# Seven block products for four of the twelve hidden tiles in a gated-attention and mixer kernel

## The chip, the cores and the metric

One NeuronCore of a Trainium2 chip runs the whole kernel. The metric is the device time of one execution in microseconds; the kernel before takes 1113.02 us, the median of three runs.

## The reference, cut to what matters

For each of 8 batches of 3008 rows and 256 channels, an attention without softmax gates u, and the result x goes through a mixer over rows (tokens) and then over channels:

```python
scores = (1 / S) * z @ z.T                   # 3008 x 3008, d_qk = 64
x      = u * (relu(scores) ** 2 @ v)         # 3008 x 256
h      = relu(x.T @ w_tok1) @ w_tok2         # tokens: 3008 -> 256 -> 3008
u2     = x + h.T
out    = u2 + relu(u2 @ w_ch1) @ w_ch2       # channels: 256 -> 1536 -> 256
```

The change is in the last line: in `u2 @ w_ch1` (the first channel product), and in how the sums for the second one are made. Operands are bf16, sums f32.

## The kernel before, in words

**Tiles.** A batch's 3008 rows are cut into 6 blocks q of 512 (the last has 448). Channels stand on the partitions as two tiles of 128 (DT = 2), the 1536 hidden channels as 12 tiles of 128 (CHT = 12). The first channel product of one block is `ch1` (line 1149): for c2 = 0 to 5 it computes two of the 12 hidden tiles, r = 0 and 1, each as two matmuls of 128 x 128 weights by 512 columns into one bank (line 1162), four matmuls a piece; six pieces a block. ScalarE evacuates the two banks in one ReLU of 1024 columns into `h2pre` (line 1201).

**The second channel product** (`product`, line 1272) already is a two-by-two block scheme with seven products in place of eight. It splits the 12 hidden tiles in halves r, the rows of a block in halves m and the 256 outputs in halves h. VectorE makes four sums of quarters of `h2pre` for each third d of the hidden tiles (`make_sums`, line 1227, operations at 1241, 1246, 1250, 1253) into `hsum`; four sums of the weights lie in `w_mix_sb` (`mix_weights`, line 974). The seven products, k = 1 to 7, are 12 matmuls of 128 columns each (line 1298) into the banks xb and zb; between them VectorE collects partial results into `ro` (`collect`, line 1309, operation at 1334). A product that goes on adding in the same bank (6 after 1, 3 after 5, 7 after 6, 4 after 7) waits for the collection of the one before it. After the seventh collection the block is stored with one DMA from SP's queue (line 1339). The token product (`tok1`, line 1008) is such a scheme too, with sums from `x_sums` (line 908).

**Banks.** PSUM is used as four pairs of banks. A piece takes a free pair (`take_slot`); the pair comes back when the operation that evacuates it is done. During a block's products xb and zb hold two of the four pairs, the pieces of `ch1` share the rest.

**What sets the order.** The program is written out by a planner in the kernel's own code. `push` (line 364) queues an operation of ScalarE, VectorE or SP with a time at which it is ready, a duration and a priority; `run_engines` gives out the earliest. TensorE's work is in pieces, in lists that are taken from the front (`next_piece`, line 1525). The planner only fixes the order of each engine's instructions; on the chip each engine runs its own list in order and waits on semaphores.

In the mixer, the pieces of a block q stand in this order (line 1510): the second product's pieces k = 1 to 7, and where a 0 stands a `ch1` piece of the next block, c2 = 0 to 4; the sixth, c2 = 5, comes just before the next block's turn:

```python
(0, 0, 1, 2, 0, 6, 5, 0, 7, 3, 0, 4)
```

Blocks 0 to 2 of a batch run in one stretch after its token product, with the `ch1` pieces of blocks 1 to 3 in between; blocks 3 to 5 follow one batch later. Attention (scores at line 465, products with v at line 692) runs in between.

Of the kernel before, what the change touches and what calls it, by code (L numbers as in the profile page):

```python
# [57 lines left out]
def kernel(  # L58
# [29 lines left out]
    sb = ctx.enter_context(tc.tile_pool(name="sb", bufs=2))  # L88
    psum = ctx.enter_context(tc.tile_pool(name="psum", bufs=2, space=bass.MemoryType.PSUM))
# [7 lines left out]
    mark = consts.tile([P, 32], F32)  # L97
# [4 lines left out]
    w_mix_sb = consts.tile([P, 4, CHT // 2, P], BF16)  # L102
    w_sum_sb = consts.tile([P, 3, KT // 2, P], BF16)
    ident = consts.tile([P, P], BF16)

    zs = consts.tile([P, KT + 2, d_qk], BF16)
# [74 lines left out]
    def turn_on_pe(zr, zp):  # L181

        for t in range(GK):
            nc.tensor.matmul(  # L184
                zp[:, t, :], zr[:, t].rearrange("p h d -> p (h d)"), ident[:],
                start=(t == 0), stop=True, skip_group_check=True)
# [15 lines left out]
    def fill(n, bank):  # L202

        for _ in range(n):
            nc.tensor.matmul(
                bank, zero[:, :P], zero[:], start=True, stop=True, skip_group_check=True)
# [672 lines left out]
    def turn_x(b, q, t):  # L879
# [10 lines left out]
        push("dve", t + slack, 0.21, 0.36, lambda t: x_sums(b, q, t), first=-1,  # L890
# [17 lines left out]
    def x_sums(b, q, t):  # L908


        if q % 2 == 0:
            d_pairs[b, q] = new_pair(xd_home(b, q), [3, QW // P // 2, P], "d_pair")
# [4 lines left out]
        steps = [(d[:, 1], high[:, 1], low[:, 1]), (low[:, 1], low[:, 1], low[:, 0]),  # L917
                 (d[:, 0], high[:, 1], low[:, 1]), (d[:, 2], high[:, 0], d[:, 0])]
# [55 lines left out]
    def mix_weights(t):  # L974
# [5 lines left out]
        for c in range(2):  # L980
# [3 lines left out]
                (to[:, 0], low[:, :, 1, :], low[:, :, 0, :]),  # L984
                (to[:, 2], high[:, :, 1, :], low[:, :, 1, :]),
                (to[:, 1], high[:, :, 1, :], to[:, 0]),
                (to[:, 3], high[:, :, 0, :], to[:, 1])]

        def step(t):
            nc.vector.tensor_sub(*steps.pop(0))  # L990
# [5 lines left out]

    BORROW = 3
    VERY_LAST = (B - 1, NQ - 1, CHT // 2 - 1)
    ORDER_LAST = ((1, 2, 6, 5, 7, 0, 3, 4), (1, 2, 6, 5, 0, 7, 3, 0, 4))

    def add_mixer(b):
# [6 lines left out]
        def tok1(q, end):  # L1008
# [10 lines left out]
            for i in range(n):  # L1019
# [4 lines left out]
                    ((1, 1), w[:, j, 0, 1, :], xp[:, 1, i, 0, :]),  # L1024
                    ((0, 2), w_sum_sb[:, 1, j, :], d[:, 0, i, :]),
                    ((1, 2), w_sum_sb[:, 0, j, :], d[:, 1, i, :]),
                    ((0, 3), w_sum_sb[:, 2, j, :], xp[:, 1, i, 1, :]),
                    ((1, 0), w[:, j, 1, 1, :], d[:, 2, i, :]),
# [8 lines left out]
            if q == NQ - 1:  # L1037
                home = "fl" if b else "h2"

                def collect_a(t):  # L1040
# [20 lines left out]
                    def one_high(t):  # L1061
                        nc.vector.tensor_add(f[:, 1, :], a_ps[:, 0, 3, :], f[:, 4, :])
                        st["a"] = sb.tile([P, 2, D], BF16, tag="a", name="a_sb", bufs=1)
# [12 lines left out]
                    def relu_a(m, t):  # L1076
# [7 lines left out]
                        if len(made) == 2:  # L1084
                            recent[0] = to[:, :1]
                            if b:
                                release("fl", [1], max(made))
                            else:
                                live["h2"] -= 1

# [8 lines left out]
        def tok2(q, end):  # L1099
# [9 lines left out]
            def add(t):  # L1109
# [13 lines left out]
                u_done[q].t = t  # L1123
                st["turned", q] = push("sp", t, 1.25, 5.5, lambda t: turn_u2(q, t), first=1,
                                       room=lambda: has_room(("us",)) and (
                                           q <= HALF or goal[0] > (b, 1 + HALF)))
            ring.append((push("dve", end + 0.21, 1.12, 1.25, add, first=2), slot))

# [20 lines left out]
        def ch1(q, c2, borrowed, end):  # L1149
# [64 lines left out]
            if c2 == CHT // 2 - 1:  # L1214
                release("xT", xT_uses[q])

# [4 lines left out]
        def tiles_of(q, d, r, m):  # L1221

            n = pairs_of(q)
            return st["h2", q, d].rearrange("p (j r) w -> p j r w", r=2)[
                :, :, r, :2 * n * P].rearrange("p j (i m s) -> p j i m s", m=2, s=P)[:, :, :, m, :]

        def make_sums(q, d, t):
# [6 lines left out]
            def kind(k):  # L1234
                return sums["s"][:, k, :, :n, :]

            def add1(t):
                home, n_home = take_home(q)
                sums["s"] = sb.tile([P, 4, 2, 2, P], BF16, tag=home, name="hsum", bufs=n_home)
                st["sum", q, d] = sums["s"]  # L1240
                nc.vector.tensor_add(kind(0), tiles_of(q, d, 0, 1), tiles_of(q, d, 1, 1))  # L1241
                push("dve", t - 0.05, busy, busy + 0.15, add3, done=s_done[q, d, 2])
# [679 lines left out]
```

## Time and profile before

| | |
|---|---|
| runs, us | 1117.03, 1112.36, 1113.02; median 1113.02 |
| span of the profiled execution | 1110.5 us (the page gives no other time of this execution) |
| instructions | 27244 |
| busy share: TensorE, VectorE, ScalarE, GpSimd | 100%, 70%, 60%, 15% |
| evacuations at line 1201 | 287, mean 1008 ns |
| stores at line 1339, from SP | 47, median 338 ns of issue |

How to read it: PE is TensorE, DVE VectorE, ACT ScalarE, POOL GpSimd, SP the engine that issues most DMAs; PEld is TensorE's weight load, SPq and ACTq are the queues of SP and ScalarE, where a DMA's issue is listed that the busy times leave out. A row of a group has line, engine, operation, output and inputs, shapes, count, then busy time and mean ns, then the idle time ahead of them and what ended it. A row of the timeline has start, length (both us), engine, line and operation; consecutive ones are merged, with their count. A row of the waits has who waited for whom, total us, times, longest. A matmul's listed duration includes its passage through the array; the next one is issued earlier.

### The profile page before, as it was taken

Reading aid. Unit: us, or ns where it says so; the run is one execution under the profiler, and the core shown is the slowest. Engines: PE = TensorE matmul, PEld = TensorE weight load, DVE = VectorE, ACT = ScalarE, POOL = GpSimd, SP = SyncE. Lnnn points to the kernel's source line nnn. Section 1 sums busy time; section 2 is a strip of 40 time slices with the busy share of each in tenths; the row PEclk is TensorE's granted clock in tenths of the full one; section 3 lists DMA queues with packets and bytes.
Section 4 is the critical chain, followed back from the end, with each engine's and each line's share of the span. In section 5 each row is a group of like instructions: output and inputs, shape, how many; then the busy total and the mean of one; then the engine's idle time right before and its main releaser. Section 6 shows DMA issues by size and latency. Waiting matters only on the chain.

```text
span 1110.5 us, 27244 instructions
## 1 busy us (share of the span) xinstructions
PE 1105.7 (100%) x11073; PEld 683.8 (62%) x11073; DVE 782.5 (70%) x1888; ACT 669.4 (60%) x843; POOL 164.3 (15%) x382
## 2 busy tenths in 40 slices
PE   9999999999999999999999999999999999999998
PEld 3444575766557665576556865557655676556676
DVE  6889865975758857588566885578756777556775
ACT  7999555645854567545665456653666536743454
POOL 5320110221003110032100311003210120000100
PEclk9999999999999999999999999999999999999999
DMA  9999947796977969779697797967979678693222
GB/s 177 155 194 164 192 98 143 141 174 134 191 133 141 180 148 174 133 147 203 135 183 119 131 214 139 172 123 152 202 154 170 111 148 182 127 164 93 67 58 96
DMA packets 465725, 165.54 MB, mean 149 GB/s; under 512 B 433024, under 2 KB 448960, under 8 KB 465600
## 3 DMA queue, kind: packets, MB, share of 16 engines
q1 hardware_dynamic: 436208, 131.11, 58.6%
q0 software_dynamic: 28880, 32.32, 21.2%
q8 instruction: 86, 1.41, 0.5%
q10 hardware_dynamic: 512, 0.38, 0.1%
q14 instruction: 39, 0.32, 0.1%
HBM read 65.40 MB, written 24.64 MB: 81 GB/s over the span
## 4 chain that ended last, share of the span: by engine, by line
PE 99%; DMA 1%; issue 0%; POOL 0%; DVE 0%; POOLq 0%
PE acc L692 42%; PE hp L1162 22%; PE xb L1298 11%; PE zb L1298 8%; PE sc L465 6%; PE h_ps L1105 4%; PE a_ps L1031 3%; PE op L1398 2%; PE first_acc L609 1%; DMA v_sb<-in_v_dram 1%; PE zp L184 0%; PE up L1700 0%; DVE res L1433 0%; POOL ident masks.py:199 0%; POOL ident masks.py:197 0%
## 5 line engine op out<-in xcount | busy, mean ns | idle before, releaser
L1201 ACT ACTIVATE h2pre<-hp 128x1024 bf16<-128x1024 f32 (+1 forms) x287 | 278.5, 1008 | 204.0 <-PE hp L1162 171.5
L692 PEld LDWEIGHTS <-v_sb 64*128 64x128 bf16 x4418 | 246.3, 94 | 210.9
L692 PE MATMUL acc<-at,v_sb 64*128 64x512 bf16 (+1 forms) x2738 | 340.9, 375 | 0.0
L503 ACT ACTIVATE at<-sc 128x1024 bf16<-128x1024 f32 (+1 forms) x290 | 286.6, 1027 | 62.5 <-PE sc L465 54.8
L1162 PE MATMUL hp<-xT,w_ch_sb 128*128 128x512 bf16 (+1 forms) x1152 | 274.7, 375 | 0.0
L511 DVE TENSOR_TENSOR at<-at 128x1024 bf16<-128x1024 bf16 (+1 forms) x290 | 198.2, 687 | 103.8 <-ACT at L503 99.9
L692 PE MATMUL acc<-fl,v_sb 64*128 64x512 bf16 (+1 forms) x1680 | 192.5, 367 | 0.0
L1162 PEld LDWEIGHTS <-w_ch_sb 128*128 128x128 bf16 x1152 | 105.6, 98 | 98.1 <-issue 3.0
L1298 PEld LDWEIGHTS <-hsum 128*128 128x128 bf16 x2088 | 124.4, 98 | 18.2 <-issue 0.3
L465 PE MATMUL sc<-zT 64*128 64x512 bf16 (+1 forms) x732 | 131.8, 359 | 0.2 <-ACT zT L1750 0.2
L1298 PEld LDWEIGHTS <-h2pre 128*128 128x128 bf16 x1566 | 95.5, 98 | 20.1
L820 ACT COPY cp<-acc 128x512 f32<-128x512 f32 (+1 forms) x94 | 54.9, 584 | 77.8 <-PE acc L692 66.8
L826 DVE TENSOR_TENSOR cp<-acc,cp 128x512 f32<-128x512 f32 (+1 forms) x94 | 63.5, 676 | 50.7 <-ACT cp L820 50.1
L1241 DVE TENSOR_TENSOR hsum<-h2pre 128x512 bf16<-128x512 bf16 (+1 forms) x141 | 56.1, 402 | 40.7 <-ACT h2pre L1201 39.4
L491 ACT ACTIVATE at<-sc 128x512 bf16<-128x512 f32 (+3 forms) x152 | 56.2, 447 | 41.5 <-PE sc L465 41.0
L1298 PE MATMUL xb<-w_mix_sb,hsum 128*128 128x128 bf16 x1044 | 73.7, 219 | 0.0
L1334 DVE TENSOR_TENSOR ro<-xb,u_sb 128x256 f32<-128x256 f32 (+1 forms) x141 | 56.5, 401 | 22.5 <-PE xb L1298 20.5
L542 DVE TENSOR_TENSOR at<-at 128x512 bf16<-128x512 bf16 (+3 forms) x152 | 41.5, 321 | 38.2 <-ACT at L491 38.2
L465 PEld LDWEIGHTS <-zT 64*128 64x128 bf16 x732 | 42.8, 94 | 41.2 <-issue 3.6
L124 POOL CAST mark<-at 128x1 f32<-128x1 bf16 x24 | 8.2, 342 | 372.5 <-DVE at L511 372.5
L846 DVE TENSOR_TENSOR xT<-cp,uT 128x512 bf16<-128x512 f32 (+1 forms) x94 | 62.5, 665 | 0.9
L1253 DVE TENSOR_TENSOR hsum<-h2pre,hsum 128x512 bf16<-128x512 bf16 (+1 forms) x141 | 56.6, 401 | 2.3
(89 smaller groups left out, 968.4 us busy)
## 6 DMA issues: line engine op xcount, KB each, us to landing
out_dram<-ro SPq DMA_DIRECT2D x40, 512.0 KB, 3.0
v_sb<-in_v_dram POOLq DMA_DIRECT2D x40, 256.0 KB, 4.6
ur<-in_u_dram POOLq DMA_DIRECT2D x40, 256.0 KB, 4.9
w_tok_sb<-in_moe_w_tok_dram POOLq DMA_DIRECT2D x10, 256.0 KB, 10.7
zs<-in_z_dram POOLq DMA_DIRECT2D x35, 64.0 KB, 3.8
at<-at SPq DMA_TRANSPOSE x114, 2.4
out_dram<-ro SPq DMA_DIRECT2D x7, 256.0 KB, 3.5
fl<-at SPq DMA_TRANSPOSE x105, 4.7
```

What stands on the lines that cost most here:

```text
L465: nc.tensor.matmul(sc[:, r, c0:c1], zT[h, k:k + P], zT[h, m + c0:m + c1], start=True, stop=True)
L491: nc.scalar.activation(a3[:, i, c0:c1], sc[:, r, c0:c1], ACT.Relu, scale=inv_S)
L503: nc.scalar.activation(view, sv, ACT.Relu, scale=inv_S)
L511: nc.vector.tensor_mul(view, view, view)
L692: nc.tensor.matmul(o, vs[blk.b, g][rows, i, dh * P:(dh + 1) * P], rhs, start=(dh, h) not in blk.begun, stop=stop, skip_group_check=True)
L826: nc.vector.tensor_add(cp[:, :W], acc[:, 0, :W], cp[:, :W])
L846: nc.vector.tensor_mul(xT[:, dh, :full * P].rearrange("p (t s) -> p t s", s=P), acc[:, :full * P].rearrange("p (t s) -> p t s", s=P), uT[: ...
L1162: nc.tensor.matmul(hps[r % len(hps)][:, r, :W], w_ch1_sb[:, dc, cc * P:(cc + 1) * P], xT[:, dc, :W], start=(dc == 0), stop=(dc == DT - 1))
L1201: nc.scalar.activation(h2[:, :, :W], hp[:, :, :W], ACT.Relu)
L1253: nc.vector.tensor_sub(kind(3), tiles_of(q, d, 1, 0), kind(1))
L1298: nc.tensor.matmul(to[:, i * P:(i + 1) * P], lhs, weights[:, c2, :], start=(first_use and c2 == 0 and i == 0), stop=(c2 == CHT // 2 - 1), ...
L1334: nc.vector.tensor_add(res(m, h), source, us(m, h) if opening else res(m, h))
```

## The change

For the batches b > 0 and the blocks q = 1, 2, 3, the first four of the 12 hidden tiles (d = 0, the pieces c2 = 0 and 1) are computed by seven block products. The block's 512 columns are halved (m, 256 each), the two channel tiles k are the inner dimension's halves, and the four hidden tiles are halved to r = 0, 1 with two tiles j each. Each of the seven products is two matmuls of 256 columns. They are given in four stages a, b, c, d, all in one pair of banks, one bank for each r (both column halves m of a product's j lie side by side in its bank):

- a: a plain product into bank 0, a mixed one into bank 1. ScalarE then copies bank 1 to a tile `s5` (`keep`) and copies bank 0 over bank 1 (`fork`).
- b: one more product into each bank. ScalarE evacuates bank 1 with a ReLU (`relu_first`) and forks again.
- c: one more into each bank. VectorE adds `s5` to both banks, with a clamp at 0, into half of `h2pre`, one operation of 1024 columns (`add_two`, the custom operation TENSOR_ADD_SAT).
- d: a last product into bank 1, evacuated by ScalarE with a ReLU (`relu_last`).

A stage waits for the work named behind the stage before it. The four mixed blocks of activations are made by VectorE in three operations per block (`token_quarters`: one of 512 columns, two of 256) into a tile `t_sums`, the mixed weights once in four operations (`hidden_weights`). The order of pieces of a block ahead of a grouped one becomes `GROUPED`; the three 0s are c2 = 2, 3, 4.

The forms of the sums change everywhere: `make_sums` makes three operations (one twice as wide) in place of four, and `x_sums` three in place of four; the signs of the weight sums and the places of the products 3, 4, 6, 7 change with them. The stores of the blocks are issued by ScalarE (`nc.scalar.dma_start`), put in its list when the planner has the last collection done. Memory: the mixed weights share one tile with the z rows, the identity shares one with the zeros, the ReLU of the token product lies in the tile of its sums, which is released after the last token piece instead of before the first.

```diff
+    HID, MIX = 8 * P, 4 * (CHT // 2) * P
+    shared_sb = consts.tile([P, HID + KT * d_qk + MIX], BF16)
+    w_hid_sb = shared_sb[:, :HID].rearrange("p (k j c) -> p k j c", k=4, c=P)
+    w_mix_sb = shared_sb[:, HID + KT * d_qk:].rearrange("p (k c d) -> p k c d", k=4, d=P)
+    zs = shared_sb[:, HID - d_qk:HID + (KT + 1) * d_qk].rearrange("p (t d) -> p t d", d=d_qk)
...
-        steps = [(d[:, 1], high[:, 1], low[:, 1]), (low[:, 1], low[:, 1], low[:, 0]),
-                 (d[:, 0], high[:, 1], low[:, 1]), (d[:, 2], high[:, 0], d[:, 0])]
+        steps = [(d[:, 0:2], v[:, 1].rearrange("p j r d -> p r j d"), low),
+                 (d[:, 2], high[:, 1], d[:, 0]), (d[:, 3], high[:, 0], d[:, 2])]
...
+    def hidden_weights(t):
+        w1 = w_ch1_sb[:, :, :4 * P].rearrange("p k (j r c) -> p r k j c", r=2, c=P)
+        to = w_hid_sb
+        steps = [
+            (nc.vector.tensor_add, to[:, 0], w1[:, 1, 0], w1[:, 1, 1]),
+            (nc.vector.tensor_sub, to[:, 1], to[:, 0], w1[:, 0, 0]),
+            (nc.vector.tensor_sub, to[:, 2], w1[:, 0, 0], w1[:, 1, 0]),
+            (nc.vector.tensor_sub, to[:, 3], w1[:, 0, 1], to[:, 1])]
...
+    GROUPED = ("a", 0, 1, 2, "b", 6, 5, 0, "c", 7, 3, 0, 4, "d")
...
+        def grouped(q, d=0):
+            return b > 0 and 0 < q <= HALF and d == 0
...
+        def token_quarters(q):
+            xT = xTs[b, q]
+            quarter = xT.rearrange("p k (m n) -> p k m n", m=2)
...
+                nc.vector.tensor_sub(tile_["T"][:, 0:2], quarter[:, :, 1], quarter[:, 0])
...
+                nc.vector.tensor_sub(T[:, 2], quarter[:, 1, 1], T[:, 0])
...
+                nc.vector.tensor_sub(T[:, 3], quarter[:, 1, 0], T[:, 2])
...
+        def grouped_ch1(q, d, stage, end):
...
+            products = [
+                [(0, w1[:, 0, 0], x[:, 0, 0], True), (1, w_hid_sb[:, 0], T[:, 0], True)],
+                [(1, w1[:, 0, 1], x[:, 1, 0], False), (0, w_hid_sb[:, 1], T[:, 2], False)],
+                [(0, w_hid_sb[:, 3], x[:, 1, 1], False), (1, w_hid_sb[:, 2], T[:, 1], False)],
+                [(1, w1[:, 1, 1], T[:, 3], False)]][stage]
+            for r, lhs, rhs, begins in products:
+                for j in range(2):
+                    nc.tensor.matmul(
+                        ps[:, r, j * 2 * P:(j + 1) * 2 * P], lhs[:, j, :], rhs,
+                        start=begins and j == 0, stop=True, skip_group_check=True)
...
+            def fork(t):
+                nc.scalar.copy(half(1), half(0))
+            def keep(t):
+                nc.scalar.copy(s5, half(1))
+                push("act", t - 0.16, 0.62, 0.78, fork, first=2, done=g_done[q, d, 0])
+            def relu_first(t):
+                nc.scalar.activation(h[:, 0, 0], half(1), ACT.Relu)
+                push("act", t - 0.16, 0.62, 0.78, fork, first=2, done=g_done[q, d, 1])
+            def relu_last(t):
+                nc.scalar.activation(h[:, 1, 0], half(1), ACT.Relu)
...
+            def add_two(t):
+                nc.vector._custom_dve(
+                    TENSOR_ADD_SAT, out=h[:, :, 1, :], in0=ps,
+                    in1=s5.unsqueeze(1).to_broadcast([P, 2, QW]), s0=3.0e38, s1=0.0)
+                make_sums(q, d, t, last=h2_done[q, 2 * d])
...
-                nc.vector.tensor_add(kind(0), tiles_of(q, d, 0, 1), tiles_of(q, d, 1, 1))
+                nc.vector.tensor_sub(sums["s"][:, 0:2, :, :n * P], h[:, :, 1], h[:, 0])
...
-                    nc.sync.dma_start(
-                        out=rows_of(out[b], q)[:, :2 * n, :], in_=st["res", q][:, :2 * n, :])
-                    free["sp"] = max(free["sp"], t) + 0.4
-                    release(home_of(q), [1], t + 4.0)
+                    push("act", t, 0.1, 0.1, store, first=1)
                     release("us", us_uses[q])
+
+            def store(t):
+                nc.scalar.dma_start(
+                    out=rows_of(out[b], q)[:, :2 * n, :], in_=st["res", q][:, :2 * n, :])
+                release(home_of(q), [1], t + 4.0)
...
+                for k in (ORDER_LAST[b % 2] if q == NQ - 1 else GROUPED if grouped(q + 1) else
+                          (0, 0, 1, 2, 0, 6, 5, 0, 7, 3, 0, 4)):
+                    if isinstance(k, str):
+                        add_grouped(q + 1, 0, "abcd".index(k), q)
```

More of the change, by code (lines that the diff above doesn't have):

```diff
@@ L205, in fill @@
             nc.tensor.matmul(
-                bank, zero[:, :P], zero[:], start=True, stop=True, skip_group_check=True)
+                bank, zero[:, :P], zero, start=True, stop=True, skip_group_check=True)
     def load_v(b, c):
@@ L1230, in make_sums @@
+        def make_sums(q, d, t, last=None):
             n = pairs_of(q)
@@ L1505, in add_mixer @@
                 add_next(q, q)
+            if q + 1 < NQ and grouped(q + 1):
+                added[q + 1] = 2
             rest = [(half, i) for half in halves(q) for i in range(pieces_of(q, half))]
@@ L1567 @@
     new_zT(0)
[L1568 to L1569 removed]
+    zero_ident = sb.tile([P, QW + P], BF16, tag="h2", name="zero", bufs=ROOM["h2"])
+    zero, ident = zero_ident[:, :QW], zero_ident[:, QW:]
+    nc.vector.memset(zero, 0.0)
     make_identity(nc, ident)
```

189 lines of the change are left out of this document (135 added, 54 removed).

## The prediction

> **What bounds the kernel now.** I read the page first: busy shares, the granted clock, the chain that ended last.
>
> ```profile
> span 1110.5 us, 27244 instructions
> ...
> PE 1105.7 (100%) x11073; PEld 683.8 (62%) x11073; DVE 782.5 (70%) x1888; ACT 669.4 (60%) x843; POOL 164.3 (15%) x382
> ...
> PEclk9999999999999999999999999999999999999999
> ...
> PE 99%; DMA 1%; issue 0%; POOL 0%; DVE 0%; POOLq 0%
> ```
>
> TensorE is busy for 1105.7 of 1110.5 us, at full clock in every slice, and is 99% of the chain. A busy TensorE need not be one that waits for nothing, so the next view is its own waits, all of them:
>
> ```profile
> PE wp L205 <- DVE zero L1569: 1.2, 1, 1.2
> PE first_acc L609 <- DMA v_sb<-in_v_dram: 0.4, 1, 0.4
> PE sc L465 <- ACT zT L1750: 0.2, 1, 0.2
> ```
>
> All three lie at the start; in the mixer it waits for nobody. So the time is the sum of the matmuls' issue times. These come from the chain in order of time, where a piece is start, length, line and count:
>
> ```profile
> 908.30 1.31 PE op L1398 x12
> 939.08 2.59 PE hp L1162 x12
> 1038.72 1.56 PE a_ps L1031 x28
> ```
>
> A matmul of 512 columns costs 2.59/12 = 0.2158 us, of 256 columns 1.31/12 = 0.1092, of 128 columns 1.56/28 = 0.0557.
>
> **The change on TensorE.** Seven batches (b > 0) times three blocks (q = 1, 2, 3) are 21 grouped blocks. In each, two pieces of line 1162 with four matmuls of 512 columns go, and seven products of two matmuls of 256 columns come: 21 x 8 = 168 go, 21 x 14 = 294 come. 168 x 0.2158 = 36.25 us go, 294 x 0.1092 = 32.10 come: **4.15 us less**, 0.198 per block. All of it is on the path, since TensorE is the path. Everything else counts only if it makes TensorE wait.
>
> **What the products wait for.** The seven products share one pair of banks in four stages a, b, c, d, and between stages ScalarE or VectorE must work on those banks. What lies between is the question. The timeline of a middle block before:
>
> ```profile
> 938.91 2.75 PE L1162 MATMUL hp<-xT,w_ch_sb 128*128 128x512 bf16 x12
> ...
> 939.15 0.42 DVE L1334 TENSOR_TENSOR ro<-xb,u_sb 128x256 f32<-128x256 f32 x1
> 939.60 0.34 SPq L1339 DMA_DIRECT2D out_dram<-ro  x1
> 939.98 2.85 ACT L1201 ACTIVATE h2pre<-hp 128x1024 bf16<-128x1024 f32 x3 [0.46 <-PE hp L1162]
> ...
> 941.03 0.43 DVE L1241 TENSOR_TENSOR hsum<-h2pre 128x512 bf16<-128x512 bf16 x1 [1.46 <-ACT h2pre L1201]
> ...
> 941.37 0.42 DVE L1250 TENSOR_TENSOR hsum<-h2pre 128x512 bf16<-128x512 bf16 x1
> 941.50 0.83 PE L1298 MATMUL xb<-w_ch_sb,h2pre 128*128 128x128 bf16 x12
> ...
> 942.17 0.83 PE L1298 MATMUL zb<-w_ch_sb,h2pre 128*128 128x128 bf16 x12
> ...
> 942.84 1.03 PE L1162 MATMUL hp<-xT,w_ch_sb 128*128 128x512 bf16 x4
> ...
> 943.70 0.83 PE L1298 MATMUL xb<-w_mix_sb,hsum 128*128 128x128 bf16 x12
> 943.95 1.02 ACT L1201 ACTIVATE h2pre<-hp 128x1024 bf16<-128x1024 f32 x1 [1.12 <-issue]
> ```
>
> A piece hp issues for 0.86 us (942.84 to 943.70), a product of the second layer for 0.67 (941.50 to 942.17). ScalarE starts 0.21 to 0.25 us after a piece's last issue (0.86 after 938.91 is 939.77, it starts at 939.98; 943.70 to 943.95): 0.23. Three evacuations take 2.85, so one follows the next after 0.92. VectorE's operations of 512 bf16 follow after 0.34.
>
> ```profile
> 927.45:937.32 9.87, 9.87 (x111) 7.03 (x109) 7.02 (x20) 5.92 (x6) 0.53 (x1) 1.00 0.78 178
> ```
>
> That is one block's cycle, 9.87 us: TensorE full, VectorE 7.02, ScalarE 5.92 (columns PE, PEld, DVE, ACT, POOL). After the change the cycle should be 9.67. The durations for the new work:
>
> ```profile
> L820 ACT COPY cp<-acc 128x512 f32<-128x512 f32 x78 | 46.3, 594 | 53.8 <-PE acc L692 53.8
> L491 ACT ACTIVATE at<-sc 128x512 bf16<-128x512 f32 x38 | 23.0, 605 | 37.4 <-PE sc L465 36.9
> L1114 DVE TENSOR_TENSOR xT<-xT,h_ps 128x1024 bf16<-128x1024 bf16 x40 | 47.5, 1217 | 4.3 <-PE h_ps L1105 3.9
> L511 DVE TENSOR_TENSOR at<-at 128x1024 bf16<-128x1024 bf16 x278 | 190.8, 690 | 102.1 <-ACT at L503 98.4 <-DMA fl<-at 0.2
> L1334 DVE TENSOR_TENSOR ro<-xb,u_sb 128x256 f32<-128x256 f32 x120 | 50.5, 421 | 16.8 <-PE xb L1298 14.7 <-issue 0.2
> L921 DVE TENSOR_TENSOR d_pair<-x_pair 128x256 bf16<-128x256 bf16 x96 | 25.5, 289 | 0.1
> ```
>
> **ScalarE** loses two evacuations of 1024 and gains five operations of 512: keep (a copy to s5), two forks (a copy from one bank to the other), relu_first and relu_last. Copy and ReLU are in the rows above, 0.59 to 0.61. The fork is not in the trace; nearest is line 820's copy, as many f32 elements from the same source, 0.594. Into a bank instead of a tile it may be shorter or longer; I take 0.60 with bounds of 0.5 and 0.7, and keep both for the range. Sum: 5.92 - 2 x 0.92 + 5 x 0.60, and 0.4 for the store below: 7.5 of 9.67 us. By the Trainium skill's page "ScalarE: Activation LUTs" (section What ACT_TABLE_LOAD costs) an instruction with immediate scale and bias takes 186 ns + 0.833 ns per element, an estimate of 0.61 for 512; two links by that are 0.03 longer than two by the row, under 0.7 us over all 21 blocks. The same page says that writing PSUM is the faster direction for ScalarE; no row here shows it.
>
> **VectorE** gains three sums of quarters (0.42, 0.29, 0.29) and add_two, a wide add of 1024 from PSUM with a broadcast f32 operand, a custom operation that the trace does not have. Nearest is line 1114, 1.22 for as many elements from PSUM; below that nothing speaks for less, above I bound it by two passes, 2.43. I take 1.22. Per d it makes three sums instead of four, 0.69 (line 511) and two of 0.42: 0.15 less, three times. 7.02 + 2.22 - 0.45 = 8.8 busy: under 9.67, so it is not the bound, but its order matters.
>
> **The tight place, step by step.** Times from the issue of stage d of the block before (0): d to 0.22, last hp to 1.08, a to 1.52, hp to 2.38, products 1 and 2 to 3.72; then b may start. ScalarE's order in the changed program is: evacuation, last ReLU, store, evacuation, keep, fork, evacuation.
> - The evacuation of the hp before product 4 starts at -0.44, the last ReLU at 0.48, ending 1.08.
> - The store waits for VectorE's collection of product 4. That one stands behind the wide add and the two 1024-wide sums: wide add 7.03 to 8.25 of the old cycle, two collections to 8.92, a quarter sum to 9.13, two wide sums to 10.36, collection to 10.71, that is 1.04. What this wait holds up is all of ScalarE's queue, and behind it stage b.
>
> ```profile
> L1339 SPq DMA_DIRECT2D out_dram<-ro x47: 332/338/538, 147.2 to 1102.4; - x47
> L163 ACTq DMA_DIRECT2D zf<-in_z_dram x3: 408/451/453, 0.8 to 1.7; - x3
> SPq L1339 <- DVE ro L1334: 185.7, 34, 14.6
> ```
>
> - The store's issue takes 0.34 on SP, and ScalarE's own issues took 0.45: it is over at 1.43 to 1.54. SP waited 185.7 us for these adds; that wait now falls on ScalarE, mostly while it would be idle.
> - The evacuation of hp starts at 1.48, keep at 2.40, fork at 3.02 to 3.62, and b can start at about 3.70. TensorE arrives at 3.72. **Margin: nothing.** If the last ReLU also has to wait for the 1024-wide sum of its tile (to 10.36, so 0.69), b is 0.1 late.
> - b to c: first ReLU at 4.4, fork 5.0 to 5.6, and TensorE arrives at 6.36: 0.7 spare. c to d: wide add done at 8.25, d starts at 9.67: 1.4 spare. Product 4 needs the collection of product 7 (8.58): it starts at 9.00, 0.4 spare. Product 6 needs the collection of product 1 (4.01): 4.16, 0.1 spare.
>
> In the first block of a batch there is no store at this place, and keep waits for the third evacuation of a row: the same working gives 0.1 spare. So I take 0.05 us of waiting for each of the 21 blocks, bounds 0 and 0.2: **1.0 us**, 0 to 4.2.
>
> **What costs nothing, and its cover.** The stores leave SP: TensorE's list of waits has no transfer of SP's in the mixer, so an earlier transpose gains nothing. Three sums instead of four in x_sums and make_sums, four sums for the hidden weights, the shared tiles and the fl buffer held longer by tok2: on VectorE, SP and memory, covered by TensorE's work; were the cover gone, the four weight sums are some 1.2 us once.
>
> **Sum.** Against the span: 1110.5 - 4.15 + 1.0 = 1107.3. The median of the runs is 1113.02, 2.5 above the span (what lies around it, and the run): 1109.9 us.
>
> **Rivals.**
> 1. The chain through ScalarE eats the gain. For it: the margin of nothing at b, and a store that waits in the same queue. Against: 2 us of ScalarE's cycle stay idle, so a delay doesn't add up from block to block. At 0.15 to 0.35 us per block it is 3.2 to 7.4 us: 1112 to 1116. Break-even is 0.2 per block.
> 2. The wide add is slow, and the kernel **slower**. Place: product 4 waits for the collection of product 7, which stands behind the add. At 2.43 us the collection ends at 9.8 instead of 9.0: 0.85 late, 21 x 0.85 = 17.9, so 1113.0 - 4.2 + 17.9 = 1126.8. It begins to cost from 1.6 us and turns the sign from 1.8. For it: an operation that the trace does not show. Against: same elements and source as 1.22.
> 3. The short matmuls cost as much as they save, because each brings its own weight load:
>
> ```profile
> L1162 PEld LDWEIGHTS <-w_ch_sb x1152: 94/98/100, 129.8 to 1101.7; 128*128 128x128 bf16 x192
> ```
>
> If the 126 additional loads of 98 ns stood open, that is 12.3 us: 1113.0 - 4.2 + 12.3 = 1121. The piece op at 908.30 speaks against it: 12 matmuls of 256, each with its load, in 1.31 us. The Trainium skill's "TensorE: Matmul & The Clock Gate" (section Back-to-back issue gap) gives sustained 81 ns for 128 columns and 131 for 512, by which short ones are dear; midway between, an estimate of 98 for 256, the change would cost 294 x 0.098 - 168 x 0.131 = 6.8 us instead of saving. The trace has 55.7 and 215.8 ns and disagrees with both figures.
> 4. The seven products bring what is counted, and no wait at all, or earlier transposes help a little: 1107.5 to 1108.7.
>
> **How the numbers follow.** Forecast (waits up to 0.15 per block, 1108.7 to 1112): 0.61. Rival 1: 0.22. Rival 2: 0.08. Rival 3: 0.03. Rival 4: 0.06. The forecast, two thirds of rival 1 and most of rival 4 give 0.8 between 1108.4 and 1114.2. About 0.5% (5.6 us) can be told from no change in a measurement of this kernel; the whole of the gain is 4.15, so faster by more has 0.02, within it 0.88 (forecast, rivals 1 and 4), slower by more (above 1118.6) 0.10 from rivals 2 and 3.
>
> **What would show it.** In the changed profile: 294 matmuls of 256 columns at 0.109 us each; a block's cycle of 9.67 to 9.75; the fork at 0.6 and the wide add at 1.2; TensorE's waits by stage: a wait for ScalarE's fork ahead of b of about 0.05 per block, none ahead of c and d, none for VectorE's collections. A wide add of over 1.6, a wait of over 0.2 ahead of b, or evacuations that start late behind the store would make the forecast wrong.

## The result and the profile after

The kernel after took 1143.03 us in the median of four runs (1131.16 to 1162.13), the kernel before 1113.32 beside it. The ratio is **1.0164, 95% interval 1.0135 to 1.0193**: slower by some 18 us. The forecast was 1109.9 us (1108.4 to 1114.2) and gave a slower kernel 0.10. The ratios leave out executions more than 1.5% above the fastest of their kernel, which are two of the four of after (1153.37 and the profiled 1162.13 us) and one of e7's four, so this profile is read for durations, order and waits, and not for its total.

The page of the kernel after:

```profile
span 1160.3 us, 27360 instructions
...
PE 1116.7 (96%) x11126; PEld 703.6 (61%) x11199; DVE 811.8 (70%) x1787; ACT 682.8 (59%) x906; POOL 164.9 (14%) x382
...
PE 80%; DMA 11%; DVE 6%; ACT 1%; issue 1%; ACTq 0%; DVEq 0%
```

TensorE was 99% of the chain and is now 80%; transfers on the DMA engines have 11% of it, VectorE 6%. So something makes TensorE wait. The first suspect is the new stage. Here are two grouped blocks in a row, from the issue of stage d to the next d (columns: busy us of PE, PEld, DVE, ACT, POOL; then clock, DMA share and GB/s):

```profile
978.53:988.20 9.67, 9.56 (x116) 7.63 (x115) 8.58 (x21) 6.67 (x10) 0.53 (x1) 1.00 1.10 222
988.20:997.87 9.67, 9.56 (x115) 7.62 (x115) 7.86 (x19) 6.65 (x10) 0.00 (x0) 1.00 0.19 65
```

The cycle is 9.67 us, as worked out (9.87 less 0.198). The pieces of the chain have the forecast lengths too, two products of two matmuls of 256 columns in 0.44 and four matmuls of 512 in 0.86:

```profile
979.77 0.44 PE gp L1313 x4
980.21 0.86 PE hp L1193 x4
```

Nor are the two operations slow that the trace of before did not have, the fork and the wide add (min/median/max in ns):

```profile
L1321 ACT COPY gp<-gp x42: 570/570/570, 257.8 to 1126.3; 128x512 f32<-128x512 f32 x42
...
L1339 DVE CUSTOM_DVE_ANT_1 h2pre<-gp,s x21: 1223/1225/1226, 262.0 to 1128.4; 128x1024 bf16<-128x1024 f32 x21
```

The loss is in other places. The three largest of TensorE's own waits (total us, times, longest; all nine come to 36 us), of which before had three of 1.2 us or less, all at the start:

```profile
PE xb L1448 <- DVE ro L1481: 17.4, 6, 5.1
PE sc L471 <- ACT at L509: 4.6, 3, 3.8
PE acc L698 <- DVE at L517: 4.3, 1, 4.3
```

And what ScalarE and VectorE themselves wait for, in two views:

```profile
ACT at L509 <- DMA fl<-at: 15.6, 6, 4.7
```

```profile
DVE hsum L1384 <- DMA out_dram<-ro: 20.1, 6, 6.0
DVE d_pair L927 <- DMA x_pair<-xT: 12.8, 7, 5.3
```

The chains behind the large waits begin with a transfer. ScalarE cannot write the next scores into an `at` buffer because the transpose that reads it is still under way; VectorE cannot make sums because the transpose into x_pair has not landed, or because the store that reads the buffer has not. In the kernel before ScalarE has no wait for a transfer at all, and VectorE's for the store is 1.0 us in sum. The transposes themselves, first before, then after (issue on SP in ns; then us from issue to landing):

```profile
L562 SPq DMA_TRANSPOSE fl<-at x105: 1381/2139/6262, 86.0 to 993.3; - x105
...
DMA to landing us min/median/max: 3.6/4.7/8.3
```

```profile
L568 SPq DMA_TRANSPOSE fl<-at x105: 1327/2559/10348, 87.0 to 1049.2; - x105
...
DMA to landing us min/median/max: 4.3/5.0/14.9
```

The same 105 transfers of the same size, which nobody changed, need 4.3 us at the least where they needed 3.6. Waiting behind other transfers could explain the longer maximum; that the quickest of 105 transfers is slower too points at the transfer itself.

A long wait can also cost more than its length. TensorE's granted clock is 0.987 on average here. After the first 10 us and up to the last matmul it stands at half in seven stretches of 3.4 or 6.8 us, 31 us in all, and each of them begins during a wait of 2.4 us or more, or within 1 us of its end; in before there is none. One such stretch, behind the wait that ends at 374.10, and the time after it (columns as above):

```profile
375.00:378.40 3.40, 3.40 (x23) 2.52 (x23) 1.49 (x5) 0.43 (x1) 0.00 (x0) 0.50 0.02 5
378.50:381.90 3.40, 3.40 (x53) 2.91 (x51) 1.75 (x6) 1.30 (x2) 1.44 (x4) 1.00 0.53 156
```

By the clock these 31 us cost some 15 (an estimate), beside the 36 us of the waits; together that is about the 50 us by which the span is longer than before.

### The profile page after: what moved, and what is told of

Same layout as the page of the kernel before. It is cut to its first block, busy times and chain, and to the rows that moved or that the text cites. A ratio compares the mean times of both kernels' runs of the same rounds, so it can differ in the third digit from the quotient of the medians.

```text
span 1160.3 us, 27360 instructions
## 1 busy us (share of the span) xinstructions
PE 1116.7 (96%) x11126; PEld 703.6 (61%) x11199; DVE 811.8 (70%) x1787; ACT 682.8 (59%) x906; POOL 164.9 (14%) x382
## 4 chain that ended last, share of the span: by engine, by line
PE 80%; DMA 11%; DVE 6%; ACT 1%; issue 1%; ACTq 0%; DVEq 0%
PE acc L698 35%; PE hp L1193 13%; PE xb L1448 8%; PE zb L1448 6%; PE sc L471 6%; DMA out_dram<-ro 4%; PE h_ps L1129 4%; DMA x_pair<-xT 3%; PE a_ps L1059 3%; PE gp L1313 2%; DMA fl<-at 2%; PE op L1547 2%; DVE ro L1481 1%; DMA u_sb<-xT 1%; DVE hsum L1384 1%; DMA at<-at 1%
## 5 line engine op out<-in xcount | busy, mean ns | idle before, releaser
L1232 ACT ACTIVATE h2pre<-hp 128x1024 bf16<-128x1024 f32 (+1 forms) x245 | 239.9, 1005 | 213.0 <-PE hp L1193 181.3
L698 PE MATMUL acc<-at,v_sb 64*128 64x512 bf16 (+1 forms) x2738 | 344.8, 376 | 6.1 <-DVE at L517 4.3
L1193 PE MATMUL hp<-xT,w_ch_sb 128*128 128x512 bf16 (+1 forms) x921 | 238.1, 377 | 3.3
L1448 PEld LDWEIGHTS <-hsum 128*128 128x128 bf16 x2088 | 130.1, 99 | 39.6 <-issue 22.1
L1193 PEld LDWEIGHTS <-w_ch_sb 128*128 128x128 bf16 x984 | 91.6, 99 | 80.1 <-issue 4.8
L1384 DVE TENSOR_TENSOR hsum<-h2pre 128x1024 bf16<-128x1024 bf16 (+1 forms) x141 | 90.0, 646 | 49.1 <-DMA out_dram<-ro 20.1
L1448 PE MATMUL xb<-shared_sb,hsum 128*128 128x128 bf16 x1044 | 74.6, 221 | 17.6 <-DVE ro L1481 17.4
L1481 DVE TENSOR_TENSOR ro<-xb,u_sb 128x256 f32<-128x256 f32 (+1 forms) x141 | 56.2, 399 | 18.0 <-PE xb L1448 15.5
## 6 DMA issues: line engine op xcount, KB each, us to landing
w_tok_sb<-in_moe_w_tok_dram POOLq DMA_DIRECT2D x10, 256.0 KB, 13.5
```

The lines of the kernel that those rows point to most:

```text
L698: nc.tensor.matmul(o, vs[blk.b, g][rows, i, dh * P:(dh + 1) * P], rhs, start=(dh, h) not in blk.begun, stop=stop, skip_group_check=True)
L1193: nc.tensor.matmul(hps[r % len(hps)][:, r, :W], w_ch1_sb[:, dc, cc * P:(cc + 1) * P], xT[:, dc, :W], start=(dc == 0), stop=(dc == DT - 1))
L1232: nc.scalar.activation(h2[:, :, :W], hp[:, :, :W], ACT.Relu)
L1384: nc.vector.tensor_sub(sums["s"][:, 0:2, :, :n * P], h[:, :, 1], h[:, 0])
L1448: nc.tensor.matmul(to[:, i * P:(i + 1) * P], lhs, weights[:, c2, :], start=(first_use and c2 == 0 and i == 0), stop=(c2 == CHT // 2 - 1), ...
L1481: nc.vector.tensor_add(res(m, h), source, us(m, h) if opening else res(m, h))
```

## The experiments

"Ratio" is against the kernel before on the same chip.

| run | what it is | median us | ratio, 95% interval |
|---|---|---|---|
| after | | 1143.03 | 1.0164, 1.0135 to 1.0193 |
| e1 | after, store on SP's queue | 1130.02 | 1.0157, 1.0127 to 1.0186 |
| e2 | before, store on ScalarE's queue | 1115.51 | 1.0032, 1.0018 to 1.0046 |
| e3 | after, no groups | 1134.66 | 1.0207, 1.0185 to 1.0229 |
| e4 | after, stored buffers given back 6 us later | 1158.31 | 1.0416, 1.0400 to 1.0431 |
| e5 | after, tiles moved up by 128 B | 1118.11 | 1.0034, 1.0020 to 1.0048 |
| e6 | e5, store on SP's queue | 1111.70 | 0.9987, 0.9975 to 0.9998 |
| e7 | before, tiles moved down by 128 B | 1125.78 | 1.0094, 1.0067 to 1.0121 |
| e8 | before, tiles moved up by 256 B | 1112.95 | 0.9994, 0.9985 to 1.0004 |
| e9 | before, transposes' sources moved by 128 B | 1119.80 | 1.0050, 1.0031 to 1.0069 |
| e10 | before, all but these moved by 128 B | 1116.93 | 1.0037, 1.0016 to 1.0058 |
| e11 | before, tiles moved down by 64 B | 1125.80 | 1.0096, 1.0066 to 1.0127 |
| e12 | e6, no groups | 1118.42 | 1.0042, 1.0021 to 1.0063 |
| e13 | e6, x_sums in four operations, old planned times | 1109.77 | 0.9977, 0.9963 to 0.9992 |
| e14 | e6, x_sums' old planned time alone | 1109.73 | 0.9968, 0.9958 to 0.9978 |
| e15 | e6 once more | 1114.05 | 1.0006, 0.9993 to 1.0020 |
| e16 | e14, no groups | 1114.95 | 1.0019, 1.0009 to 1.0029 |
| e17 | e14, store on ScalarE's queue | 1113.28 | 1.0007, 0.9987 to 1.0027 |
| e18 | e14, addresses of after | 1131.98 | 1.0176, 1.0147 to 1.0206 |

### First round: the store, the groups, the sums

Three theories stood after the first look. S: the store, now issued from ScalarE, lands late and holds up the sums. X: the sums, in another form and with other planned times, stand elsewhere in the order, in batch 0 above all. G: the groups cost more than they save.

e1 puts the store back:

```
-                    push("act", t, 0.1, 0.1, store, first=1)
+                    nc.sync.dma_start(
+                        out=rows_of(out[b], q)[:, :2 * n, :], in_=st["res", q][:, :2 * n, :])
+                    free["sp"] = max(free["sp"], t) + 0.4
+                    release(home_of(q), [1], t + 4.0)
```

> The changed kernel with one part undone: the blocks' stores are issued by SP again. Theory S (the store on ScalarE's queue lands late beside SP's transposes, the buffer that it reads is not free, VectorE's next sum waits for it and TensorE behind it): the waits of hsum for out_dram go, and the grouped blocks' 4 us show: 1108 to 1112 us. Theory X (the wider sums stand at other places of VectorE's order and wait for transposes in batch 0): still 1122 or more. Theory G (the grouped blocks cost more than they save): still 1130.

e2 is the opposite edit, alone, in the kernel before:

> The kernel before with one part alone: the blocks' stores are issued by ScalarE. Theory S: 1125 to 1133 us, with waits of hsum for out_dram as in the changed kernel. Theories X and G: 1113, as before.

e3 turns the groups off:

```
-            return b > 0 and 0 < q <= HALF and d == 0
+            return False
```

> The changed kernel without the grouped blocks (all twelve hidden tiles by eight products again; stores and wider sums stay). Theory G: 1113 or less. Theories S and X: about 4 us above the changed kernel, 1133 to 1137 us, the same waits.

e4 leaves the planner more time before a stored buffer is used again:

```
-                release(home_of(q), [1], t + 4.0)
+                release(home_of(q), [1], t + 10.0)
```

> The changed kernel with one number changed: the planner counts a stored buffer as free 10 us after the store's turn, not 4. Theory S: no sum is put behind a store that has not landed; the waits of hsum for out_dram (20.1 us in 6 in the changed kernel's profile) go, 1112 to 1120 us. Theory X: 1125 or more. Theory G: 1130.

G falls: without groups the kernel is no faster (1.0207 against 1.0164). S is a small part: the store's move costs the kernel before 0.32%, and to undo it in after changes the ratio from 1.0164 to 1.0157, within both intervals. How the move costs is not shown: in e2's trace TensorE already loses 3.7 of the 50 us between 75 and 125 us, while the first store is issued at 152 us, and up to 138 us every engine has the instructions of the kernel before in the same order. What differs there is that transfers land later, the loads of w_ch after 17.4 us in the median against 13.5. X stays open here (e1 and e3 came out as it says) and comes back in the fourth round. e4 shows that the planner has no buffers to spare: VectorE's wait for the store is gone from its list, and TensorE instead waits 20.2 us, seven times, in the second token product (line 1129) for ScalarE's a_f (line 1111), whose tile comes from the same buffers. What e1, e3, e4 and after share, and before and e2 do not, is a minimum of 4.2 to 4.3 us for the fl transposes, against 3.6.

### Second round: the addresses

This gave theory A. A transpose's own speed had changed, so something about its operands had. The change touches none of these transposes, but it resizes tiles that lie ahead of them. The mark tile (128 B per partition) moves to a pool of its own behind all others, and w_mix (6144), zs (3328) and ident (256) are replaced by shared_sb (11264): 11264 - 9856 = 1408 B more. In the built programs the working pool begins at byte 72192 = 141 x 512 of a partition before, and at 73600 = 143 x 512 + 384 after. Since all its tags, but for the two zT tiles of 6400 B, are multiples of 512 B, every at, fl, xT and ur tile began at a multiple of 512 before and begins 384 B past one after. Theory R, against it: the cause is the order that follows from the new sums and shared tiles.

e5 and e6 move the tiles of after up by 128 B. There is not that much room in the partition, so 32 of the 128 columns of each half of the ut tile go into the padding, at the price of four more small copies and four more adds in the whole kernel:

```
+    ut_pad = consts.tile([P, DT, 32], BF16)
...
-                    pair["ut"] = sb.tile([TAIL, DT, P], BF16, tag="ut", name="ut", bufs=1)
+                    pair["ut"] = sb.tile([TAIL, DT, P - 32], BF16, tag="ut", name="ut", bufs=1)
```

> The kernel after, with every tile behind the weights moved 128 B up per partition, so that the tiles of the working pool begin at multiples of 512 B as in the kernel before, instead of 384 B past one. Theory A (addresses: transposes on the DMA engines are slower where their tiles begin off a multiple of 512 B): 1110 to 1114 us, which is the kernel before (1113.3) less some 4.5 for the groups plus some 3.5 for the store; landings of the transposes back at the least values of before, 3.6 us for fl and 2.7 for x_pair (4.3 and 3.2 in after). Theory R (the re-made sums, the shared tiles and the order that follows from them): 1131 to 1143 as in after, landings as in after.

> The same with the store back on SP's queue. Theory A: 1107.5 to 1110.5 us, faster than the kernel before by the groups' 4 to 5 us. Theory R: about 1130, as with the store on SP and the addresses of after.

e7 and e8 do the reverse to the kernel before, which keeps all its instructions and their order:

```
-    mark = consts.tile([P, 32], F32)
+    mark = marks.tile([P, 1], F32)
```

> The kernel before, with its small mark tile moved behind the working pool, so that every other tile begins 128 B lower (384 B past a multiple of 512, as in after); the instructions are the same. Theory A: 1127 to 1136 us (ratio 1.013 to 1.02), landings of fl at least 4.2 us and of x_pair at least 3.0. Theory R: 1112 to 1115, landings as in the kernel before.

```
-    mark = consts.tile([P, 32], F32)
+    mark = consts.tile([P, 96], F32)
```

> The kernel before, with its mark tile 256 B larger, so that every tile behind it begins 256 B past a multiple of 512. Theory A, if multiples of 512 count: 1120 to 1136 us; if multiples of 256 are enough: 1112 to 1115. Theory R: 1112 to 1115.

R falls as the main cause and A holds, though three times miss their ranges: e5 came out at 1118.11, above the expected 1114, e6 at 1111.70, above 1110.5, and e7 below the expected range. The fourth round takes up what is left. With the same instructions e7 is 0.94% slower than the kernel before, e8 is not slower. The row of SP's DMA queue, which holds the transposes (packets, MB, share of the 16 engines' span), in before, e7 and e8:

```profile
q1 hardware_dynamic: 436208, 131.11, 58.6%
```

```profile
q1 hardware_dynamic: 436208, 131.11, 63.3%
```

```profile
q1 hardware_dynamic: 436208, 131.11, 58.9%
```

Equal packets and bytes, but 63.3% of 1122.0 us against 58.6% of 1110.5: 9% more time in e7. The engines are untouched: ScalarE's largest group takes as long per instruction in e7 as in before, and only the wait is new (the groups of before, then of e7; behind the bar the idle time ahead of them):

```profile
L503 ACT ACTIVATE at<-sc 128x1024 bf16<-128x1024 f32 (+1 forms) x290 | 286.6, 1027 | 62.5 <-PE sc L465 54.8 <-issue 1.1 <-DVE xT L846 1.0
```

```profile
L504 ACT ACTIVATE at<-sc 128x1024 bf16<-128x1024 f32 (+1 forms) x290 | 285.9, 1028 | 69.5 <-PE sc L466 48.1 <-DMA fl<-at 15.5 <-issue 1.1
```

The wait for `DMA fl<-at`, 15.5 us in ten pieces, is the one found in after, made by an address alone.

### Third round: read or written, and how far off

e9 puts an unused tile of 128 B ahead of the first at tile in the kernel before; e10 does that too and moves the mark tile as e7 does, so that the two halves of the pool change roles:

```
+            if not ats:
+                sb.tile([P, P // 2], BF16, tag="gap", name="gap", bufs=1)
             ats[b, q, g] = sb.tile([P, GK * QW], BF16, tag="at", name="at", bufs=ROOM["at"])
```

> The kernel before, with an unused tile of 128 B ahead of the at tiles, so that at, xT, u_sb and the two own uT tiles begin 128 B past a multiple of 512 and all others as in the kernel before; same instructions. If a transpose is slow by where it reads (at for fl, xT for x_pair): landings of fl at least 4.2 us and of x_pair at least 3.0, 1120 to 1128 us as with everything shifted (1125.8). If it is slow by where it writes: fl 3.6 and x_pair 2.7 as in the kernel before, only u_sb (3.1) and two of the uT tiles slow, 1112 to 1116 us. Theory R (order of the sums): 1113.

> The opposite: the mark tile behind the pool, so that weights, zT, x_pair, fl and ur begin 384 B past a multiple of 512, and the unused tile ahead of at, so that at, xT, u_sb and the own uT tiles begin at multiples of 512. By reading: fl 3.6, x_pair 2.7, 1112 to 1116 us. By writing: fl at least 4.2, x_pair at least 3.0, 1120 to 1128 us. If both count, fl lies between 3.6 and 4.3 in this run and the one before.

In e11 the mark tile is 64 B smaller:

> The kernel before, with every tile behind the mark 64 B lower (448 B past a multiple of 512). If all that counts is whether a tile begins at a multiple of 256: 1120 to 1132 us, landings as with 128 B (fl 4.3, x_pair 3.0). If what counts is how far it is off: landings above those, over 1135 us. Theory R: 1113.

The fl transposes of e9 (at shifted, fl not) and of e10 (fl shifted, at not):

```profile
L564 SPq DMA_TRANSPOSE fl<-at x105: 1333/2472/5520, 86.2 to 1005.1; - x105
...
DMA to landing us min/median/max: 4.3/5.1/9.1
```

```profile
L565 SPq DMA_TRANSPOSE fl<-at x105: 1376/2103/5952, 86.0 to 996.4; - x105
...
DMA to landing us min/median/max: 3.7/4.6/9.7
```

The uT transposes read ur, which lies in the other half, and 44 of the 48 uT tiles lie in the half of at, so they must turn round if the source decides. In e9 (ur at its old place) and in e10 (ur shifted):

```profile
L265 SPq DMA_TRANSPOSE uT<-ur x47: 1231/1553/2987, 19.1 to 1013.2; - x47
...
DMA to landing us min/median/max: 2.7/3.8/7.1
```

```profile
L266 SPq DMA_TRANSPOSE uT<-ur x47: 1232/1275/3184, 18.9 to 1004.6; - x47
...
DMA to landing us min/median/max: 3.1/3.5/10.7
```

They do. **It is where a transpose reads that counts.** The minimum of x_pair (from xT) is 3.0 in e9 and 2.7 in e10: with fl and uT, three transposes turn with their source and against their target. That of u_sb (from xT) is 3.1 and 2.7, but its tile moves together with xT, so it fits and decides nothing. One kind does not follow: the 114 smaller transposes of an at tile into itself (at<-at, 128 to 384 columns instead of 2048) have a minimum of 2.3 us in the kernel before and of 2.2 in e7, e9 and e11. e11's landings are those of e7 (fl 4.3, u_sb 3.1) and its ratio 1.0096 is e7's: a source 64 B short of a multiple of 512 (e11), 128 B past one (e9) or 384 B past one (e7) costs the same per transpose, and 256 B past one costs nothing (e8). So in these runs the sources of fl, x_pair, u_sb and uT are fast at a multiple of 256 B and slow at the three other places tried. The Trainium skill's page "DMA: Bandwidth & Descriptors" (section DMA Transpose (X-bar), Constraints) asks for 32-byte alignment in SBUF. Every address here meets that, so it tells what is allowed and not what is fast.

Not all adds up in the times: e9 lies just below its range, and e10, whose fl, x_pair and u_sb are fast again, is still at 1.0037 (interval from 1.0016), though its profiled span is 1112.4 against 1110.5. The 0.50% of e9 and the 0.37% of e10 together come near the 0.94% of e7, where all sources are shifted, but what the slow uT transposes of e10 cost was not taken apart.

### Fourth round: what is left

e6 mends addresses and store and gains 0.13%, where the forecast's terms say 0.28% (3.15 of 1113). e12 takes its groups away:

> The version that is realigned and stores from SP's queue, with no block taken as a group: what is left of the change is the sums of VectorE in three operations instead of four, the shared tiles, the first token product's tile held in its f buffer. If these cost nothing (as forecast): 1112 to 1115 us, and the groups are worth 1.5 to 4 us against it. If they cost what the groups' saving lacks (1.25 us measured in place of 3.15 forecast): 1114 to 1118, and the groups are worth 3 to 5.

At 1.0042 it lies above the kernel before (and at 1118.42 us just above both ranges), so something else in the change still costs. The stretch where batch 0 runs shows where, in before, e6 and e14 (below); TensorE's busy time is the first number behind the comma:

```profile
75.00:125.00 50.00, 50.00 (x518) 26.08 (x516) 44.74 (x100) 40.76 (x47) 4.21 (x10) 1.00 1.13 176
```

```profile
75.00:125.00 50.00, 47.81 (x496) 25.14 (x494) 42.43 (x91) 39.83 (x47) 3.33 (x6) 1.00 1.03 160
```

```profile
75.00:125.00 50.00, 50.00 (x518) 26.01 (x516) 44.41 (x97) 40.79 (x47) 3.92 (x10) 1.00 1.05 165
```

e6 loses 2.2 us there; no grouped block and no store run yet. The change gives x_sums three operations, the first twice as wide, and tells the planner so; e13 takes both back, e14 only the planned time, e15 repeats e6 beside them:

```
-        push("dve", t + slack, 0.34, 0.48, lambda t: x_sums(b, q, t), first=-1,
+        push("dve", t + slack, 0.21, 0.36, lambda t: x_sums(b, q, t), first=-1,
```

> The version that is realigned and stores from SP's queue (0.9987 of the kernel before), with x_sums again in four operations of 256 columns and with the planned times of the kernel before. Theory X (x_sums' other times shift the planner's order in batch 0, where TensorE loses 2.2 us between 75 and 125 us): TensorE busy at least 49.5 of these 50 us, 1108.5 to 1110.5 us, ratio 0.996 to 0.9975. If x_sums is not the cause: 1111 to 1112.5, and the 2.2 us stay.

> The same version with x_sums in three operations, and only its first planned time as in the kernel before (0.21 in place of 0.34). If the planned time alone moves the order: as theory X, 1108.5 to 1110.5 us and no loss between 75 and 125 us. If the operation's own 0.42 us in place of 0.29 does it, or neither: 1111 to 1112.5.

> The version that is realigned and stores from SP's queue once more, unchanged, beside the two others: 1110.5 to 1112.5 us, ratio 0.9975 to 0.9998, 2.2 us of TensorE lost between 75 and 125 us.

The planned time alone does it: e14 keeps the wide operation (0.42 us) and has TensorE full in that stretch, 0.9968 of the kernel before against 0.9987 of e6 and 1.0006 of e15. The truer price makes a worse order in batch 0; which operation comes too late by it was not followed.

e15 is e6 unchanged, and yet it lies above its range. Both have the one long wait of TensorE at line 472, which ends at 112 us (2.2 us in e6's trace, 2.0 in e15's). Behind it the granted clock falls to half in e15 and not in e6, first e6, then e15:

```profile
113.00:116.40 3.40, 3.40 (x62) 3.21 (x59) 3.25 (x6) 1.76 (x3) 0.00 (x0) 1.00 1.23 270
```

```profile
113.00:116.40 3.40, 3.40 (x36) 3.40 (x34) 3.25 (x6) 1.37 (x2) 0.00 (x0) 0.50 1.46 252
```

In the same 3.4 us there are 36 matmuls in place of 62. The granted clock is 0.998 in nine of e15's twelve executions and in three of e6's ten. Those at 1.0 agree: 1110.86 to 1112.25 us in e15, 1110.53 to 1112.71 in e6. So what an execution pays for this wait is not always the same: the wait alone, or the slower matmuls behind it as well.

All of TensorE's waits in e14:

```profile
PE wp L212 <- DVE zero L1738: 1.2, 1, 1.2
PE sc L472 <- DMA zT<-zr: 0.6, 1, 0.6
```

**e14 is faster than both kernels**: 1109.73 us. From it, each part was put back or taken away by itself:

> The mended version (realigned, store on SP's queue, x_sums planned at 0.21; 0.9968 of the kernel before) with no block taken as a group. If only the groups gain, by the forecast 3.15 us: 1112 to 1113.5 us, ratio 0.999 to 1.0005. If the sums in three operations still cost something that the groups hide: 1114 to 1117.

> The mended version with its stores on ScalarE's queue. By what the store's move cost the kernel before (1.0032): 1112.5 to 1114.5 us, ratio 0.9985 to 1.001, TensorE below 49 of the 50 us between 75 and 125. By the difference of the two realigned versions before x_sums was mended (1.0034 against 0.9987): 1114 to 1116. If the store costs nothing, as forecast: 1109.5 to 1110.

> The mended version with the addresses of after (384 B past a multiple of 512). By what the shift cost the kernel before (1.0094): 1119 to 1123 us, ratio 1.0055 to 1.009. If a fuller use of the buffers makes it cost more here (1.0157 with the store on SP, before x_sums was mended): 1123 to 1129. fl lands in 4.3 us at the least.

- Groups: 1.0019 without, 0.9968 with, so 0.51% or 5.7 us; by the profiled spans 1111.8 to 1107.7, 4.1 us. Without its groups the mended version is still 0.19% above the kernel before (interval from 1.0009), so the rest of the change costs some 2 us; which part of it was not taken apart.
- Store on ScalarE's queue: 1.0007 (0.9987 to 1.0027), some 0.4% lost. In e17's profile, which is of its fastest execution, TensorE's further waits are 0.9 and 0.5 us, both at line 1449; between 75 and 125 us it is full, against the expectation, and VectorE waits for the store 1.7 us in all, in e14 2.3. A store lands after 2.6 us at the least when ScalarE issues it (after, e2, e17) and after 2.1 from SP (before, e14). That the move costs is shown three times, by e2, by e5 against e6 and by e17 against e14, 0.3 to 0.5%; how it comes about is not. The same page of the Trainium skill (section Issuing engines are not separate DMA queues) says that another issuing engine saves issue time alone; these runs agree that it buys nothing here.
- Addresses: 1.0176 with those of after, 2.1% or 23 us lost, more than either expectation. The chain of e18, and what ScalarE waits for:

```profile
PE 84%; DMA 9%; DVE 4%; issue 1%; ACT 1%; SPq 0%; ACTq 0%; DVEq 0%
```

```profile
ACT at L509 <- DMA fl<-at: 19.8, 7, 3.8
```

With the old addresses the other two parts vanish in the noise: after 1.0164, e1 1.0157 and e18 1.0176 cannot be told apart. With the addresses of before, and nothing else mended, after stands at 1.0034 (e5). So **most of the slowdown is the addresses**, and the other two parts show only once these are mended. Why one shift costs the kernel before 0.94% and e14 2.1% is open. TensorE's listed waits come to 8.1 us in e7 and to 14.8 in e18. e18 has 8.9 us of VectorE waiting for `DMA x_pair<-xT`, e7 only 2.6, so the new sums have less time to spare there; that was not tested. The price of the address also isn't the transposes' own added time, 105 x 0.7 = 74 us for fl alone; most of that must stay hidden, since the kernel loses 10 to 23 us.

## Why the prediction was wrong

The forecast was a gain of 3.15 us, and the kernel lost some 18. By its own steps:

- **The change on TensorE: right.** 168 matmuls of 512 columns against 294 of 256, and a cycle of 9.67 us measured for 9.67 forecast.
- **What the products wait for: right in size.** The fork took 0.570 us (taken: 0.60, bounds 0.5 to 0.7), the wide add 1.225 (taken: 1.22). The nearest rows were good prices for operations that the trace did not have.
- **The tight place: too dear.** The margin of nothing at stage b was enough. The rows of the 294 grouped matmuls list 0.0 us of idle time in e14 and 0.3 in after, so the 1.0 us was not paid: the groups gained 4.1 us by the spans of e16 and e14 (5.7 by the ratios), for 4.15 counted.
- **The rivals: none of them.** The chain through ScalarE did not close, the wide add was not slow, the short matmuls' weight loads stayed hidden. The slower outcome had a chance of 0.10, for two reasons that were both false (the sum of rival 2 also comes to 1126.7, not 1126.8).
- **What costs nothing, and its cover: this step failed, three times.** "The shared tiles ... covered by TensorE's work" took a tile's size as free because nothing computes in it; the size moved all tiles behind it, and the transposes' reads became slow: 2.1% in e18 against e14. "Three sums instead of four in x_sums" cost nothing as an operation, but its planned time moved the order of batch 0, 2.2 us of TensorE in e6. "The stores leave SP ... gains nothing" was right that nothing is gained, and set the loss at zero: 0.3 to 0.5%.

The cover was also read wrongly. TensorE had no waits in the mixer, and the forecast took that as room. It showed only that every transfer was in time, not by how much. Of the `at` buffers there are six, and 0.7 us more per transpose was enough for ScalarE to wait for them. The page of before also has the two large DMA queues at 58.6% and 21.2% of the 16 engines' time, 80% together; the prediction shows no row of them.

With the three side effects mended the change gains 0.32% (e14, interval 0.22 to 0.42), and the forecast's 3.15 us are 0.28%. That this is so close is partly luck: inside it the groups gain 0.51% and the rest loses 0.19% (e16), where the forecast had 4.15 us of gain and 1.0 us of waiting for the fork.

## What to carry to other kernels

When a change resizes, splits or moves any tile, compare where the tiles behind it begin, before reading anything else; a pool that was aligned by luck loses that with one small tile. A transfer that nobody touched and whose *minimum* has grown was the sign here. Behind a wait of TensorE, look at its granted clock: the wait can cost more than its length. And where a planner sets the order, a new planned time is a change of its own: try it apart from the operation.

## What the runs showed of the hardware

- DMA transposes that read SBUF at a multiple of 256 B of a partition land in 3.6 to 3.7 us (fl), 2.7 (x_pair), 2.7 (uT) and 2.7 to 2.8 (u_sb) at the least; 128 B past such a multiple or 64 B short of one, in 4.2 to 4.3, 3.0 to 3.2, 3.0 to 3.2 and 3.1 to 3.2. Where fl, x_pair and uT write made no difference to these minima (e9, e10), and the smaller at<-at stay at 2.2 to 2.3 either way. The same 131.11 MB in the same packets took 63.3% of the DMA engines' time instead of 58.6% (e7, before).
- After the first 10 us and up to the last matmul, TensorE's granted clock fell to half only at waits: in nine traces, each time during a wait of 2.0 us or more or within 2 us of its end, for 3.4 or 6.8 us. Not every such wait is followed by it (2.2 us in e6, 2.6 in e11).
- ScalarE copies 512 f32 from one PSUM bank to another in 570 ns, less than the 594 ns of line 820's copy into SBUF. VectorE's custom wide add with a broadcast operand takes 1225 ns for 1024 elements, as much as the plain one (1217).
